# A gated mix of linear attention and a ReLU layer: the engines' programs written without a block

## The chip, the cores and the metric

The kernel runs on one core of a Trainium2 chip. Five engines work side by side, each with a program of its own: TensorE (PE) multiplies matrices, VectorE (DVE), ScalarE (ACT) and GpSimd (POOL) do the elementwise work and the reductions, and SyncE (SP) issues transfers. They meet through semaphores. ACT issues transfers too. The metric is the device time of one execution in microseconds.

## The reference

The input x has 2048 rows of 512. Two branches are computed from it and mixed with a gate for each row:

```
g = sigmoid((x * gate_w).sum(-1))
q, k, v = x @ wqkv, in 32 heads of 16
phi(t)  = concat(softmax(t @ w_phi), softmax(-(t @ w_phi)))     per head, for q and k
kv = phi(k)^T v ;  z = sum of phi(k)
a  = (phi(q) kv) / (phi(q) z + 1e-6) @ wo
b  = relu(x @ w1) @ w2                                          w1: 512 x 1376
out = g * a + (1 - g) * b
```

All inputs and the output are bf16.

## The kernel before

**Tiling.** The 2048 rows are 16 tiles of 128, in four chunks of 512. x stands transposed in SBUF (XT): the first chunk is turned by TensorE, the other three by transposing loads. The hidden layer HT is computed 512 rows at a time in 11 pieces of the hidden width (L397, L403, L409), and ACT applies the ReLU as it empties PSUM (L460). The projections of q and k are first folded with w_phi (L374) and then made two tiles at a time (L502). DVE takes maxima and minima, POOL subtracts them, ACT takes the exponential, DVE sums it, POOL normalizes. v is L482, the state kv is L563. The second half runs tile by tile: the attention's numerator and denominator (L606), a transposing transfer, eleven matmuls with w2 (L628) and four with wo (L634) into the same PSUM bank, one eviction scaled with the gate (L679), one store (L682). The last tile is cut into columns 0 to 351 and 352 to 511, with matmuls on L649 and L660: ACT evicts and stores the first part (L667, L673), DVE evicts the second part (L670) and SP stores it (L673).

**What sets the order.** Each piece of work is a task with a name, an engine and the tasks that it depends on. The order of the tasks on each engine is written out by hand in `ORDER`. `emit` walks an engine's list, puts a wait (L144) ahead of a task where a semaphore has to reach a value, writes the task's instructions and lets the last one count the engine's semaphore up. A transfer has a semaphore of its own, which reaches 16 when it has landed.

**Around the programs.** Before the kernel's function is called, the program object has already written a preamble (the profile shows it under L732): POOL writes four small constants, and all engines meet in a barrier. The function ends with five programs, one for each engine, written inside a block (`nc.Block()`). A block gives every engine a section of its own, which the engine enters with a branch and leaves with a branch to a common end. At that end each engine drains, and all engines meet in a barrier; the profile shows these records under L188, the line of the function itself. In SP's section, `emit` is followed by waits for the stores of the last tiles: stores 9 to 14 (L700) and the two stores of tile 15 (L702). Earlier stores have been waited for by the tasks that reuse their buffers.

A barrier of this kind goes so: SP, ACT, PE and DVE each drain and count one semaphore up; POOL drains, waits until that semaphore is at 4, and sets a second semaphore; the others wait for that and count it down.

Of the kernel before, what the change touches and what calls it, by code (L numbers as in the profile page):

```python
# [148 lines left out]
def bass_gated_mix__linear_kernel_hedgehog__dense_activation_relu__prompt_kernel(  # L149
# [17 lines left out]
    NT = S // P  # L167
# [13 lines left out]
    NPH, NOM, NOT, NOS = 7, 3, 4, 5  # L181
# [6 lines left out]
    with ExitStack() as es:  # L188
        E = es.enter_context
# [52 lines left out]
        g = _Graph()  # L242
# [444 lines left out]
        order = g.schedule()  # L687
        g.number(order)
        sems = {e: nc.alloc_semaphore(f"s_{e}") for e in ENGINES}
        for t in g.tasks.values():  # L690
            if t.dma:
                sems[t.sem] = nc.alloc_semaphore(f"d_{t.name}")
        block = E(nc.Block())

        @block.sync
        def _(q):
            g.emit("sp", q, order, sems)

            for m in range(NT - NOS - 2, NT - 1):
                q.wait_ge(sems[f"st{m}"], 16)  # L700
            for hf in range(2):
                q.wait_ge(sems[f"st{NT - 1}_{hf}"], 16)  # L702

        @block.gpsimd
        def _(q):
            g.emit("pool", q, order, sems)

        @block.scalar
        def _(q):
            g.emit("act", q, order, sems)  # L710

        @block.vector
        def _(q):
            g.emit("dve", q, order, sems)

        @block.tensor
        def _(q):
            g.emit("pe", q, order, sems)


# [26 lines left out]
```

## Time and profile before

| | |
|---|---|
| device time, median of 3 runs | 151.53 us (151.14, 151.53, 152.31) |
| span of the profiled execution, first to last instruction | 150.2 us |
| the profiled execution's own time | not given beside the span; the median is 1.33 us above the span |
| PE busy | 145.2 us (97%) |
| DVE, POOL, ACT busy | 113.4, 109.4, 92.2 us |
| granted clock of TensorE | 1.000 |

Busy times count work on the engine's data path. Waits on semaphores, branches, drains and the issuing of transfers are done by an engine's sequencer and are not counted as busy; views of a single source line list them with their durations and starts. A name with a q behind it (SPq, ACTq) is a sequencer.

### The profile page before, as it was taken

To read this page: it belongs to the slowest core of one execution; us is meant where nothing else is said; L and a number is where in the kernel's file an instruction comes from. 1 tells how busy PE (TensorE), PEld (TensorE's weight loads), DVE (VectorE), ACT (ScalarE), POOL (GpSimd) and SP (SyncE) were. 2 spreads that over 40 slices of the span, in tenths; PEclk is the share of its full clock that TensorE was granted. 3 is DMA by queue.
4 is the path that set the end of the run, shared out by engine and by line. 5 is a ranking of instruction groups with operands and counts; after the bars stand their busy time and mean duration, and the time that the engine had idled before them with its cause. 6 is when DMAs were issued, how large, how long until landed. Compare 5 with 4: busy or idle time off the path is not lost.

```text
span 150.2 us, 2515 instructions
## 1 busy us (share of the span) xinstructions
PE 145.2 (97%) x944; PEld 74.2 (49%) x961; DVE 113.4 (76%) x168; ACT 92.2 (61%) x127; POOL 109.4 (73%) x71
## 2 busy tenths in 40 slices
PE   7899999999999999999999999999999999999992
PEld 3664444445554465445444545445444454454461
DVE  2433666999899949979999899999999969436301
ACT  3356769799969766698983937446546551310151
POOL 3000499999999999999999999998999791330000
PEclk9999999999999999999999999999999999999999
DMA  4999995000005602300000230476698774986251
GB/s 146 280 179 233 213 203 108 0 0 0 7 1 132 218 4 66 103 0 0 4 0 0 56 86 18 92 175 140 174 110 173 179 209 105 109 212 140 64 162 53
DMA packets 46307, 15.59 MB, mean 104 GB/s; under 512 B 39796, under 2 KB 46292, under 8 KB 46296
## 3 DMA queue, kind: packets, MB, share of 16 engines
q1 hardware_dynamic: 43560, 12.99, 42.0%
q10 hardware_dynamic: 2736, 2.45, 5.1%
q8 instruction: 7, 0.11, 0.4%
q14 instruction: 4, 0.03, 0.1%
HBM read 4.42 MB, written 2.11 MB: 43 GB/s over the span
## 4 chain that ended last, share of the span: by engine, by line
PE 93%; DMA 3%; issue 1%; ACT 1%; SPq 1%; DVE 0%
PE PS L628 24%; PE PS L397 23%; PE PS L502 18%; PE PS L482 9%; PE PS L634 9%; PE PS L563 3%; PE PS L606 3%; DMA W<-in_B_w_dram 3%; PE PS L649 2%; PE PS L374 1%; ACT HT L460 1%; PE PS L403 1%; PE PS L660 1%; SPq L272 1%; PE PS L409 0%
## 5 line engine op out<-in xcount | busy, mean ns | idle before, releaser
L542 POOL TENSOR_TENSOR TS<-PB,MX 128x1024 bf16<-128x1024 bf16 (+1 forms) x18 | 30.9, 1723 | 14.9 <-DVE MX L533 14.9
L397 PE MATMUL PS<-XT,W 128*128 128x512 bf16 (+1 forms) x156 | 38.3, 379 | 0.2
L628 PE MATMUL PS<-W,HT 128*128 128x512 bf16 (+1 forms) x160 | 37.5, 379 | 0.3
L549 DVE TENSOR_REDUCE ZB<-FT 128x128 f32<-128x2048 bf16 (+1 forms) x18 | 36.6, 2031 | 1.0 <-ACT FT L547 1.0
L547 ACT ACTIVATE FT<-TS 128x2048 bf16<-128x2048 bf16 (+1 forms) x18 | 30.9, 1718 | 7.7 <-POOL TS L542 7.5
L542 POOL TENSOR_TENSOR TS<-MN,PB 128x1024 bf16<-128x1024 bf16 (+1 forms) x18 | 30.9, 1724 | 0.8 <-DVE MN L535 0.8
L502 PE MATMUL PS<-WP,XT 128*128 128x512 bf16 x124 | 30.0, 379 | 0.2
L556 POOL TENSOR_TENSOR FT<-FT,SC 128x2048 bf16<-128x2048 bf16 (+1 forms) x9 | 29.5, 3290 | 0.0
L460 ACT ACTIVATE HT<-PS 128x512 bf16<-128x512 f32 (+1 forms) x44 | 24.7, 597 | 5.8 <-PE PS L397 4.9
L628 PEld LDWEIGHTS PS<-W,HT 128*128 128x128 bf16 (+1 forms) x165 | 15.5, 98 | 17.1
L533 DVE TENSOR_REDUCE MX<-PB 128x64 bf16<-128x1024 bf16 (+1 forms) x18 | 19.5, 1085 | 5.8 <-ACT PB L529 5.7
L397 PEld LDWEIGHTS PS<-XT,W 128*128 128x128 bf16 (+1 forms) x160 | 15.6, 101 | 16.5
L679 ACT ACTIVATE OSB<-PS,OMG 128x512 bf16<-128x512 f32 x15 | 10.2, 687 | 20.3 <-PE PS L634 20.3
L535 DVE TENSOR_REDUCE MN<-PB 128x64 bf16<-128x1024 bf16 (+1 forms) x18 | 19.3, 1084 | 2.3 <-ACT PB L529 2.3
L529 ACT ACTIVATE PB<-PS 128x1024 bf16<-128x1024 f32 (+1 forms) x18 | 16.7, 927 | 6.7 <-PE PS L502 3.8
L502 PEld LDWEIGHTS PS<-WP,XT 128*128 128x128 bf16 x128 | 12.1, 98 | 13.9 <-DVE WP L344 0.4
L579 POOL TENSOR_TENSOR FT<-FT,SR 128x1024 bf16<-128x1024 bf16 (+1 forms) x9 | 15.6, 1739 | 0.7
L482 PE MATMUL PS<-WV,XT 128*128 128x512 bf16 x62 | 16.0, 379 | 0.1
L634 PE MATMUL PS<-WO,OT 128*128 128x512 bf16 x58 | 14.2, 378 | 0.1
L615 DVE SCALAR_TENSOR_TENSOR OTM<-PS,EG,RD 128x256 bf16<-128x256 f32 x32 | 13.8, 463 | 0.2
L613 DVE RECIPROCAL RD<-PS 128x16 f32<-128x16 f32 x32 | 6.5, 235 | 9.0 <-PE PS L606 8.8
L491 ACT ACTIVATE VS<-PS 128x512 bf16<-128x512 f32 x16 | 9.6, 603 | 4.8 <-PE PS L482 4.7
(50 smaller groups left out, 97.8 us busy)
## 6 DMA issues: line engine op xcount, KB each, us to landing
out_dram<-OSB ACTq DMA_DIRECT2D x15, 128.0 KB, 2.1
W<-in_B_w_dram SPq DMA_DIRECT2D x1, 1280.0 KB, 6.7
W<-in_B_w_dram SPq DMA_DIRECT2D x1, 512.0 KB, 5.6
WV<-in_A_wqkv_dram SPq DMA_DIRECT2D x1, 512.0 KB, 4.7
WO<-in_A_wo_dram SPq DMA_DIRECT2D x1, 512.0 KB, 4.7
FT<-in_A_x_dram SPq DMA_DIRECT2D x3, 128.0 KB, 4.0
W<-in_B_w_dram SPq DMA_DIRECT2D x1, 352.0 KB, 3.9
W<-in_B_w_dram ACTq DMA_DIRECT2D x2, 128.0 KB, 3.7
```

The costliest lines, as they stand in the source:

```text
L397: last = q.matmul(PS[0:m, b, :], W1[:, j, k * P:k * P + m], XT[:, j, chunk(c)], start=(j == 0), stop=(j == ND - 1))
L460: add(f"rl{a}_{k}", "act", lambda q, a=a, k=k, b=b, rows=rows: q.activation(HT[0:rows, k, chunk(a)], PS[0:rows, b, :], ACT.Relu), (prev,), ...
L482: last = q.matmul(PS[:, 2, :], XT[:, j, m * P:(m + 1) * P], WV[:, j, :], start=(j == 0), stop=(j == ND - 1))
L502: last = q.matmul(PS[:, n, :], XT[:, j, m * P:(m + 1) * P], WP[:, s, j, :], start=(j == 0), stop=(j == ND - 1))
L533: add(f"mx_{J}", "dve", lambda q, sl=sl, w=w, i=pbg: q.tensor_reduce(MX[:, sl, 0:w * H], i, AX.X, ALU.max), (f"ev_{J}", old("t1")), dur=0. ...
L535: add(f"mn_{J}", "dve", lambda q, sl=sl, w=w, i=pbg: q.tensor_reduce(MN[:, sl, 0:w * H], i, AX.X, ALU.min), (f"ev_{J}", old("t2")), dur=0. ...
L542: add(f"{tn}_{J}", "pool", lambda q, o3=o3, a3=a3, b3=b3: q.tensor_tensor(o3, a3, b3, ALU.subtract), (f"{'mx' if sg == 0 else 'mn'}_{J}", ...
L547: add(f"ex_{J}", "act", lambda q, fs=fs, ts=ts, w=w: q.activation(FT[:, fs, 0:w * F], TS[:, ts, 0:w * F], ACT.Exp), (f"t1_{J}", f"t2_{J}", ...
L549: add(f"sm_{J}", "dve", lambda q, fs=fs, sl=sl, w=w: q.tensor_reduce(ZB[:, sl, 0:2 * w * H], FT[:, fs, 0:w * F].rearrange("p (g d) -> p g ...
L556: add(f"nm_{J}", "pool", lambda q, f3=f3, sl=sl, w=w: q.tensor_tensor(f3, f3, SC[:, sl, 0:2 * w * H].unsqueeze(2).to_broadcast([P, 2 * w * ...
L628: last = q.matmul(PS[:, ab, :], HT[0:r, k, m * P:(m + 1) * P], W2[0:r, k, :], start=(k == 0), stop=False)
L634: last = q.matmul(PS[:, ab, :], OT[:, m % NOT, t, :], WO[:, t, :], start=False, stop=(t == ND - 1))
```

## The change

The block goes. The five programs are written one after the other on the engines' own handles, behind the preamble. What each engine is told to do inside its program is the same, in the same order. On each engine the branch into the section and the branch to the common end go, and with the common end its drain and its part of the closing barrier go: four instructions fewer on each of SP, ACT, PE and DVE, five fewer on POOL. SP's waits on the stores stay, at the end of SP's program; the compiler packs the eight semaphores into four wait instructions, where before they were on four wait instructions and the branch. The opening barrier of the preamble stays.

```diff
-        block = E(nc.Block())
-
-        @block.sync
-        def _(q):
-            g.emit("sp", q, order, sems)
-
-            for m in range(NT - NOS - 2, NT - 1):
-                q.wait_ge(sems[f"st{m}"], 16)
-            for hf in range(2):
-                q.wait_ge(sems[f"st{NT - 1}_{hf}"], 16)
-
-        @block.gpsimd
-        def _(q):
-            g.emit("pool", q, order, sems)
...
-        @block.tensor
-        def _(q):
-            g.emit("pe", q, order, sems)
+        for e, q in (("sp", nc.sync), ("pool", nc.gpsimd), ("act", nc.scalar), ("dve", nc.vector), ("pe", nc.tensor)):
+            g.emit(e, q, order, sems)
+
+        for m in range(NT - NOS - 2, NT - 1):
+            nc.sync.wait_ge(sems[f"st{m}"], 16)
+        for hf in range(2):
+            nc.sync.wait_ge(sems[f"st{NT - 1}_{hf}"], 16)
```

More of the change, by code (lines that the diff above doesn't have):

```diff
@@ L692, in bass_gated_mix__linear_kernel_hedgehog__dense_activation_relu__prompt_kernel @@
                 sems[t.sem] = nc.alloc_semaphore(f"d_{t.name}")
-        block = E(nc.Block())
-        @block.sync
-        def _(q):
-            g.emit("sp", q, order, sems)
-            for m in range(NT - NOS - 2, NT - 1):
-                q.wait_ge(sems[f"st{m}"], 16)
-            for hf in range(2):
-                q.wait_ge(sems[f"st{NT - 1}_{hf}"], 16)
-        @block.gpsimd
-        def _(q):
-            g.emit("pool", q, order, sems)
-        @block.scalar
-        def _(q):
[L710 to L714, printed above, removed]
-        @block.tensor
-        def _(q):
-            g.emit("pe", q, order, sems)
+        for e, q in (("sp", nc.sync), ("pool", nc.gpsimd), ("act", nc.scalar), ("dve", nc.vector), ("pe", nc.tensor)):
[4 more added lines that the diff above has]
+            nc.sync.wait_ge(sems[f"st{NT - 1}_{hf}"], 16)
 _INS = ['A_x', 'A_wqkv', 'A_w_phi', 'A_wo', 'B_x', 'B_w1', 'B_w2', 'gate_w']
```

## The prediction

> **What bounds the kernel now.** I read the page's sums first, then the chain that ended last, and then three answers on the two ends of the span, because the change touches nothing between them.
>
> ```profile
> span 150.2 us, 2515 instructions
> PE 145.2 (97%) x944; PEld 74.2 (49%) x961; DVE 113.4 (76%) x168; ACT 92.2 (61%) x127; POOL 109.4 (73%) x71
> PE 93%; DMA 3%; issue 1%; ACT 1%; SPq 1%; DVE 0%
> ```
>
> PE is busy for 97% of the span and makes up 93% of the chain. The chain in order of time shows where it is not PE:
>
> ```profile
> 0.67 0.07 issue
> 0.74 0.41 SPq L272
> 1.15 0.07 issue
> 1.21 0.41 SPq L272
> 1.62 0.05 issue
> 1.67 4.06 DMA W<-in_B_w_dram
> ...
> 5.87 0.60 PE PS L403 x4
> ...
> 146.44 0.89 PE PS L660 x8
> 147.33 0.03 issue
> 147.35 0.38 DVE OSB L670
> ```
>
> The reader is to see three stretches. Up to 0.67 us the opening barrier of the engines is under way (the preamble, which both kernels have). From there to 5.87 SP issues loads and PE waits for the third of them. From 5.87 to 147.33 PE works with hardly a gap. The chain stops at 147.35 + 0.38 = 147.73, yet the span is 150.2: some 2.5 us at the end belong to no compute engine. The busy times by stretch confirm it:
>
> ```profile
> 0.74:5.87 5.13, 4.70 (x26) 2.33 (x27) 1.72 (x4) 2.05 (x3) 1.25 (x4) 1.00 0.70 214
> 5.87:147.30 141.43, 140.53 (x918) 71.91 (x935) 111.32 (x163) 89.83 (x124) 107.99 (x63) 1.00 0.48 102
> 147.30:150.20 2.90, 0.01 (x1) 0.00 (x0) 0.38 (x1) 0.33 (x1) 0.00 (x0) 1.00 0.15 45
> ```
>
> After the length of the stretch the columns are PE, weight loads, DVE, ACT, POOL, the granted clock, the DMA share and GB/s. In the middle stretch PE is busy 140.53 of 141.43 us at a granted clock of 1.00. In the last one nothing computes but two evictions. What fills it stands in the timeline and in the issues of the last stretch:
>
> ```profile
> 147.66 0.35 ACTq L673 DMA_DIRECT2D out_dram<-OSB  x1
> 147.76 0.36 SPq L673 DMA_DIRECT2D out_dram<-OSB  x1
> ```
>
> ```profile
> q10 hardware_dynamic: 305, 0.23, 16.2%
> q1 hardware_dynamic: 144, 0.04, 4.0%
> issues: line engine op xcount, KB each, median us to landing
> out_dram<-OSB ACTq DMA_DIRECT2D x1, 88.0 KB, 1.6
> out_dram<-OSB SPq DMA_DIRECT2D x1, 40.0 KB, 1.7
> ```
>
> The last two stores land at 147.66 + 1.6 = 149.3 and 147.76 + 1.7 = 149.5 us. SP waits for them (L702), and only then comes the block's end (L188):
>
> ```profile
> L702 SPq EVENT_SEMAPHORE  x2: 28/28/28, 149.3 to 149.5; - x2
> ```
>
> ```profile
> L188 POOLq EVENT_SEMAPHORE  x2: 17/17/17, 149.7 to 149.8; - x2
> L188 POOLq DRAIN  x1: 1166/1166/1166, 131.7 to 131.7; - x1
> L188 PEldq DRAIN  x1: 1757/1757/1757, 145.6 to 145.6; - x1
> L188 DVEq DRAIN  x1: 422/422/422, 147.4 to 147.4; - x1
> L188 ACTq DRAIN  x1: 153/153/153, 148.0 to 148.0; - x1
> L188 SPq COMPARE_BRANCH  x1: 33/33/33, 149.5 to 149.5; - x1
> L188 SPq DRAIN  x1: 13/13/13, 149.7 to 149.7; - x1
> L188 ACTq EVENT_SEMAPHORE  x1: 17/17/17, 149.9 to 149.9; - x1
> L188 DVEq EVENT_SEMAPHORE  x1: 21/21/21, 149.9 to 149.9; - x1
> L188 PEldq EVENT_SEMAPHORE  x1: 51/51/51, 149.9 to 149.9; - x1
> L188 SPq EVENT_SEMAPHORE  x1: 17/17/17, 150.1 to 150.1; - x1
> ```
>
> In each row stand the shortest, median and longest duration in ns and the first and last start. SP is the last to arrive at the closing barrier, at 149.7: the other four had drained at 132.8 (131.7 + 1.166), 147.4, 147.8 and 148.2. Of these rows, then, only SP's road from 149.5 to 150.2 is on the path that sets the end.
>
> **The change part by part.**
>
> *The five opening branches.* Each engine's program ends its preamble with a jump into the block. In the trace the barrier's release on SP ends at 0.67 and the first load is issued at 0.74: a gap of 0.07 us that would hold the branch. Between the first and the second load, where no branch stands, the gap is also 0.07 (1.15 to 1.21). There is no branch record of any engine at the start either; SP's of L188 is the only one I find. So I cost the opening at nothing. Its bounds are 0 and the whole gap of 0.07 us, a gain that would pass fully to the end, since SP's issues head the chain and PE has no slack from 5.87 on (141.43 − 140.53 = 0.9 us idle in all). SP and ACT would lose the same branch, so their loads keep their order. The other side would be a load that starts earlier into transfer engines already 0.70 busy in that stretch, which can make the gain zero but hardly a loss.
>
> The Trainium skill, "Advanced Engine Details and Errata", section Control Flow Timing, gives about 51 ns for an unconditional branch. The trace disagrees for the start, where nothing is left of the 0.07 us once the ordinary gap between two issues is taken off. By the page the opening would give an estimated 0.05 us more.
>
> *The waits on the stores.* They stay, but pair differently. Before, SP has eight semaphores to wait for in five instructions, the last of them (store 9) on the branch itself; after, four instructions hold two each. A wait on two takes 28 ns in the rows of L702. The last one in the changed kernel waits for the same late landing (149.5) as L702's second one now, so it again ends at 149.5. Nothing is queued behind these waits on SP. Store 9 has landed before: tile 14's eviction waits for it too (it takes over the buffer of tile 9), ahead of ACT's last store at 147.66. Its wait costs nothing in either place. No wait is added on the other engines.
>
> *The closing branch, drain and barrier.* They go. Step by step on SP: branch and drain from 149.5 to 149.7, some 0.2 us, of which 0.033 + 0.013 are the instructions themselves; POOL's gathering of the four and its release, from 149.7 to the others' starts at 149.9, 0.2 us; SP's own release comes at 150.1, 0.2 to 0.3 us after the other engines'. To the end of the span that is 150.2 − 149.5 = 0.7 us. The view of SP's waits has the part after its drain as one number:
>
> ```profile
> SPq L188 <- SPq L188: 0.5, 1, 0.5
> ```
>
> Nothing hides these 0.7 us, as all five engines stand in them: the stores have landed and no compute is left. And nothing is late next inside the span, because the four other engines end before 148.3, over a microsecond ahead of SP. The span should thus end with SP's last wait, at 149.5.
>
> *What lies around the span.* The page gives the profiled execution's span but no time of its own; the median of 151.53 is 1.33 us above the span of 150.2, and no view shows those 1.33 us. I take them as a constant that begins when SP is done. Bounds: of the 0.7, the 0.3 by which SP is late in its release may be SP's own slowness after it wakes, and come back in the first thing it does after the span (gain 0.4); or the whole meeting of the engines is done over again outside (gain 0). On the other side the four engines could do their part of the 1.33 us early (gain 0.7 + 1.33 = 2.0). I stay at 0.7, the nearest row.
>
> The Trainium skill, "Runtime: NRT & Kernel Launch", section The launch sequence, says that after the kernel a synchronization of all engines follows that the runtime adds, some 1.5 us long, and then a reset of semaphores. No run here shows it. By that page the block's barrier is one of two in a row, and dropping it saves its own length and no more, an estimated 0.7 us, with no early reset.
>
> **Sum**: 0 (opening) + 0 (waits) − 0.7 (closing) = a span of 149.5 and, with the 1.33 us around it, 150.8 us: 0.46% less. That is below 1%, about what a measurement of this kernel tells from no change (the runs of before alone lie between 151.14 and 152.31).
>
> **The rivals.**
>
> *A: the meeting is only moved.* The engines still have to be gathered before the time is stopped, and the closing barrier's 0.5 us after SP's drain are paid after the span. For it: SP is late by 0.2 to 0.3 where nothing of the kernel holds it. Against it: nothing in these rows is work that anyone needs. It gives 151.0 to 151.5. If the compiler or the runtime put a closing of its own in place of the block's, so that the change doesn't do what it says, it is the same 151.5.
>
> *B: the four engines finish what follows under the stores.* POOL could enter it 17 us early, PE, DVE and ACT 1.3 to 2 us early (149.5 against 147.4 to 148.2). If most of the 1.33 us is each engine's own tidying, it disappears: 149.5 to 150.3 us, at the edge of it over 1% faster. Against it: SP is the last and must do its own part after 149.5.
>
> *C: slower, by loading of program code.* The page and an answer for a stretch late in the kernel show transfers of kind "instruction":
>
> ```profile
> q8 instruction: 7, 0.11, 0.4%
> q14 instruction: 4, 0.03, 0.1%
> ```
>
> ```profile
> q8 instruction: 1, 0.02, 3.4%
> ```
>
> Seven took 0.4% of 16 × 150.2 us, some 1.4 us each; the single one between 127 and 130.5 us took 3.4% of 16 × 3.5 = 1.9 us. Now SP stands 0.5 us at the barrier, and code that comes after can be fetched meanwhile. Without the barrier it runs on at once; and with two branches and the closing gone, every engine's program is shorter, so borders between loaded pieces fall elsewhere. If SP's next piece is asked for only when SP gets there, one load replaces the barrier: 1.4 to 1.9 minus 0.7 makes 152.2 to 152.7; two in a row, on two engines that hand on to each other, 154.1 at most. It decides from the point where the load takes longer than the 0.7 saved. Against it: between 146 and 150.2 us the queues in the rows above are q10 and q1 alone, so SP jumped to the block's end with no load at all, and it stands in waits from 148.2 on, long enough for a load.
>
> The same section's neighbour in that page of the Trainium skill, Instruction fetch mechanics, warns that a taken branch out of the loaded window stalls on a fetch. That would add to the gain, by an estimated load of 1.4 us. The trace speaks against it for the one branch that it shows, as no instruction queue is listed around 149.5.
>
> **How the numbers follow.** The forecast (gain 0.4 to 0.8, 150.7 to 151.1) has 0.68; A 0.12; B 0.13; C 0.07. The time is the forecast's, 150.8. The range runs from 150.0, in the middle of B, to 151.6, over all of A; it leaves out half of B, at 149.5 to 150.0, and C, with room for the scatter of before's runs. Over 1% faster is below 150.0: half of B and some scatter of the forecast, 0.13. Over 1% slower is above 153.0: two loads in a row in C, and scatter, 0.05. Within 1%: 0.82.
>
> **What would show it.** In the changed kernel's trace: no record on the function's own line for branch, drain or barrier after the last store; SP's last record a wait on two semaphores of about 28 ns near 149.5; a span of 149.4 to 149.6; the first load still 0.07 us after the opening barrier; PE's stretch from first dense matmul to last within 0.2 us of 141.4; no instruction load after 146 us. If the span falls by 0.7 and the time doesn't, A holds; if the time falls by far more than the span, B; if the span ends later with SP's wait records spread out, or an instruction packet stands there, C. I am wrong altogether if PE's stretch changes length, which nothing in the diff should do.

## The result, and the profile after

The changed kernel takes 151.25 us (median of 22 runs, 150.58 to 151.90), the kernel before 151.96 us (22 runs, 151.14 to 152.43). The ratio is 0.9957, with a 95% interval of 0.9944 to 0.9970: 0.43% less, where 0.46% was forecast. The median of before is 0.43 us higher than the one from three runs that the prediction started from, so both times stand higher by about that; the difference, 0.71 us, is the 0.7 of the prediction.

The page of the changed kernel has a shorter span and nearly the same busy times:

```profile
span 149.8 us, 2503 instructions
PE 145.8 (97%) x944; PEld 74.8 (50%) x961; DVE 113.6 (76%) x168; ACT 92.1 (62%) x127; POOL 109.4 (73%) x71
```

The two ends of its chain in order of time:

```profile
0.67 0.07 issue
0.74 2.90 DMA FT<-in_A_x_dram
3.63 0.05 issue
3.68 1.04 PE PS L350 x8
...
146.75 0.89 PE PS L660 x8
147.64 0.02 issue
147.67 0.38 DVE OSB L670
```

The opening is what it was: 0.07 us from the barrier to the first load. The end of PE's work is at 147.64, 0.31 later than before, and everything behind it is later by as much. The last stretch, by the timeline, and then SP's waits and what is left after them:

```profile
147.97 0.35 ACTq L673 DMA_DIRECT2D out_dram<-OSB  x1
148.08 0.36 SPq L673 DMA_DIRECT2D out_dram<-OSB  x1
```

```profile
L699 SPq EVENT_SEMAPHORE  x2: 28/28/28, 149.6 to 149.8; - x2
```

The reader is to see that the span now ends with SP's last wait, which starts at 149.8: behind it there is no record of any engine. From the issue of the last store to the end of the span it is 149.8 − 148.08 = 1.7 us, against 150.2 − 147.76 = 2.4 before. That is the 0.7 us.

**A second measure.** Each execution has a time and a span. Their difference, "time minus span", is what lies around the span, and it varies little: 1.50 to 1.61 us over 30 runs of the kernel before and 1.35 to 1.60 over 22 of the changed one, while the spans themselves scatter by over a microsecond (149.0 to 150.4 in the same 22 runs). So the spans' medians and the time minus span tell more than the time alone:

| | span, median | time minus span, median |
|---|---|---|
| before (30 and 31 runs beside the experiments) | 150.4 | 1.56 and 1.55 |
| after (22 runs) | 149.8 | 1.51 |

### The profile page after: what moved, and what is told of

Its sections match the earlier page's. It is cut to its first block, busy times and chain, and to the rows that moved or that the text cites. A ratio compares the mean times of both kernels' runs of the same rounds, so it can differ in the third digit from the quotient of the medians.

```text
span 149.8 us, 2503 instructions
## 1 busy us (share of the span) xinstructions
PE 145.8 (97%) x944; PEld 74.8 (50%) x961; DVE 113.6 (76%) x168; ACT 92.1 (62%) x127; POOL 109.4 (73%) x71
## 4 chain that ended last, share of the span: by engine, by line
PE 95%; DMA 2%; ACT 1%; issue 1%; DVE 0%
PE PS L628 24%; PE PS L397 23%; PE PS L502 18%; PE PS L482 9%; PE PS L634 9%; PE PS L563 3%; PE PS L606 3%; DMA FT<-in_A_x_dram 2%; PE PS L403 2%; PE PS L649 2%; PE PS L374 1%; PE PS L350 1%; ACT HT L460 1%; PE PS L660 1%; PE PS L409 1%
```

## The experiments

All of them start from the changed kernel, the last one from the kernel before; each computes the whole reference. The first four ran side by side on one chip, the last four on another; before ran beside both. Its medians there are 151.97 us both times.

### The changed kernel again

> The changed kernel once more, beside the other three, as their common measure and for a second trace. Expected: ratio to before 0.9957 within 0.0015; span near 149.8, its last record a wait of SP; time minus span again 1.5 us. If the first 3 us of loading differ from trace to trace by some 0.3 us with the same issue times, the difference of the two first traces in that stretch is scatter and no work of the change.

Measured: 151.30 us (12 runs), ratio 0.9951 (0.9929 to 0.9973), span 149.8, time minus span 1.47. Its chain begins in another way:

```profile
0.74 0.41 SPq L272
1.15 0.06 issue
1.21 0.42 SPq L272
1.63 0.05 issue
1.68 4.67 DMA W<-in_B_w_dram
6.36 0.14 issue
6.49 0.60 PE PS L403 x4
```

With the loads issued at the same times as in before (0.74, 1.21, and the third at 1.68 against 1.67), the third one lands 0.6 us later. The end of PE's work moves with such landings: 147.33, 147.64 and, in this trace, 147.9. In the three traces that is scatter of the loading. It explains why a single trace has its span 0.3 us off the forecast.

### One barrier, without a block

```diff
             nc.sync.wait_ge(sems[f"st{NT - 1}_{hf}"], 16)
+        nc.all_engine_barrier()
```

> The changed kernel with one barrier of all engines written behind SP's waits: the meeting is back, the block and its branches are not. Theory, the meeting of the engines is what was saved: ratio to before back to 1.000 within 0.0015, span 0.5 to 0.7 us longer than without it. Rival, the branches were what cost (SP's into the end of the block, and the five at the opening): the ratio stays at 0.996 to 0.997, as the barrier without branches costs 0.2 us or less.

Measured: 152.00 us (12 runs), ratio 1.0013 (0.9978 to 1.0047). The meeting takes the gain back, and no branch is needed for that. But the span's median is 150.15, shorter than before's 150.4, and time minus span is 1.83, longer than before's 1.56. SP stands in the meeting for less time than in before (0.5):

```profile
SPq L701 <- PEq L701: 0.2, 1, 0.2
```

So the time is as expected, and the way in which it divides isn't. This asked for the last experiment below.

### Five barriers

```diff
+        for _ in range(5):
+            nc.all_engine_barrier()
```

> The same with five barriers in a row, to read the price of one meeting from four more. By the closing meeting in the trace of before (0.5 us from SP's drain to its release): 4 x 0.5 = 2.0 us over one barrier, ratio to before 1.013; at 0.7 us each 2.8 us and 1.018. Rival, much of the first one's price is that SP or another engine comes out of it late, and a meeting of engines that stand there already costs 0.2 to 0.3 us: 0.8 to 1.2 us more, ratio 1.005 to 1.008.

Measured: 153.54 us (7 runs), ratio 1.0092 (1.0058 to 1.0127); span 151.5, time minus span 1.99. Four more meetings cost 1.54 us over one, 0.39 each: between what the two theories gave. SP's releases in the trace are 1.8 us apart from first to last, 0.44 each on average:

```profile
L702 SPq DRAIN  x5: 7/7/121, 149.1 to 150.7; - x5
L702 SPq EVENT_SEMAPHORE  x5: 17/17/17, 149.2 to 151.0; - x5
```

The four steps between them are not alike: by the starts in the trace file, which has nanoseconds, they are 0.76, 0.33, 0.33 and 0.36 us. In the first of them SP's drain begins only 0.47 us after its release; why, the trace does not show. A meeting of engines that stand there already thus costs about 0.33 us, near what the rival gave, and 0.4 with the slow one averaged in. The 0.7 of the block's end is more than either.

### The four other engines held, without a barrier

```diff
+        done = nc.alloc_semaphore("s_done")
+        nc.sync.sem_inc(done, 1)
+        for q in (nc.gpsimd, nc.scalar, nc.vector, nc.tensor):
+            q.wait_ge(done, 1)
```

> The changed kernel, but POOL, ACT, DVE and PE each end with a wait for a semaphore that SP counts up behind its waits on the stores: no drain, no gathering, but the four leave the program after SP, as in before. If what counts is only the span: span longer by 0.1 to 0.2 us (SP's count and the four waking), time minus span unchanged at 1.5, ratio 0.9967. Rival, engines that leave early also shorten what follows the span: time minus span rises to about 1.7, time 0.3 to 0.4 us over the changed kernel, ratio 0.998.

Measured: time minus span 1.93 (12 runs, 1.80 to 2.08), against 1.47 beside it: what follows the span takes 0.46 us longer when the four leave after SP, with no drain and no gathering. The time, 151.40 us, ratio 0.9966 (0.9943 to 0.9989), is only 0.1 above the changed kernel's, since the spans of this program happen to be shorter (149.55, with SP's additional work in them). The trace has no work that could make them shorter; its two waits of L699 stand at 149.7 and 149.9, as in the others, and its own execution was a long one (151.92). I count this as scatter from program to program, which no run here shows, and read the time minus span alone. By the time alone this run would show next to no loss.

### PE held, POOL held

The same edit for one engine, `nc.tensor` or `nc.gpsimd`.

> The changed kernel, but PE alone ends with a wait for a semaphore that SP counts up with its last wait on the stores; POOL, ACT and DVE leave early. Read by two measures: span, and time minus span (1.5 us in the changed kernel, 1.92 with all four held). Theory, what follows the span passes through the engines one after the other with PE at the beginning of the line: PE alone costs most of it, time minus span 1.75 to 1.9. Rival, it takes whichever engine is late at the same price: a quarter of the 0.42, so 1.6. Rival, another engine is the one that counts: 1.5.

> The same with POOL held instead of PE. Theory of a line that begins with PE: POOL stands further back in it, time minus span 1.6 to 1.7. Rival, POOL is the slow one by itself: 1.8 to 1.9 and PE less. Rival, equal shares: 1.6 for both.

Measured: with PE held 151.92 us (10 runs), ratio 0.9991 (0.9964 to 1.0017), time minus span 1.69; with POOL held 152.04 us (10 runs), ratio 1.0001 (0.9977 to 1.0025), time minus span 1.97 (1.89 to 2.01). POOL's whole record behind SP's last wait is this:

```profile
L703 POOLq EVENT_SEMAPHORE  x1: 17/17/17, 149.7 to 149.7; - x1
```

One wait of 17 ns on one engine, and by the time the whole gain is gone. By time minus span it costs 0.46 us; the rest lies in the spans, whose medians (150.05, and 150.3 with PE held) differ from program to program by more than the traces show work for. The prices that went with the line fail: PE costs 0.2, POOL 0.45 to 0.5, as much as all four together (1.93). POOL's rival is the one that holds: POOL is slow by itself. The line itself stands in the traces, with PE at its head (see the account). DVE and ACT were not tried alone.

### The waits on the stores at the end of PE

```diff
-            nc.sync.wait_ge(sems[f"st{m}"], 16)
+            nc.tensor.wait_ge(sems[f"st{m}"], 16)
...
-            nc.sync.wait_ge(sems[f"st{NT - 1}_{hf}"], 16)
+            nc.tensor.wait_ge(sems[f"st{NT - 1}_{hf}"], 16)
```

> The changed kernel with the waits on the stores at the end of PE's program in place of SP's; SP leaves with its last store. No count from SP to another engine is in the way here. Theory of a line that begins with PE: time minus span as with PE held, 1.75 to 1.9, and so 0.3 us slower than the changed kernel, ratio to before 0.998. Rival, the place of the waits is indifferent: time minus span 1.5, ratio 0.9955.

Measured: 151.93 us (10 runs), ratio 0.9978 (0.9950 to 1.0006), span 150.05, time minus span 1.88 (1.83 to 1.94). The place of the waits isn't indifferent: on SP they are cheaper by 0.37 us of time minus span. That the value is above the 1.69 of PE held, though PE ends last in both, I can't account for.

### The block with its branch freed of the wait

```diff
                 q.wait_ge(sems[f"st{NT - 1}_{hf}"], 16)
+            q.nop(nofuse=True)
```

In the trace the eight waits now stand in four records of 28 ns ahead of the branch, the last of them on the new line:

```profile
L703 SPq EVENT_SEMAPHORE  x1: 28/28/28, 149.8 to 149.8; - x1
```

> The kernel before, with its block, its branches and its closing barrier, but with SP's waits on the stores closed off ahead of the branch, so that four instructions hold them all and the branch to the end holds none. Theory, SP's late release in before (0.2 to 0.3 us after the other engines') comes of that one branch: without a wait on it SP is released with the others, the span is 0.3 us shorter (150.1), time minus span grows from 1.56 to 1.83 as with one barrier and no block, and the time is unchanged, ratio 0.999 to 1.001. Rival, the block's end itself makes SP late: span and time minus span as in before.

Measured: 151.96 us (10 runs), ratio 0.9995 (0.9974 to 1.0017); span 150.1, 0.3 shorter than before's; time minus span 1.82 (1.80 to 1.89), 0.27 longer. The records of the block's end:

```profile
L188 SPq DRAIN  x1: 7/7/7, 149.9 to 149.9; - x1
L188 SPq EVENT_SEMAPHORE  x1: 17/17/17, 150.1 to 150.1; - x1
L188 ACTq EVENT_SEMAPHORE  x1: 17/17/17, 150.1 to 150.1; - x1
L188 PEldq EVENT_SEMAPHORE  x1: 51/51/51, 150.1 to 150.1; - x1
```

There is no branch record on SP any more, and SP is released with the others. In before, the branch that carried a wait cost SP some 0.3 us inside the span, and the time nothing: other engines were still on the way by then, as time minus span shows and the account makes plain.

### The account

"Tail" is from the start of SP's (or PE's) second wait on the stores of tile 15 to the end of the time: what is left of the span there by the trace, and the median time minus span. The views give starts to 0.1 us; the two decimals are from the trace files.

| | span left | time minus span | tail |
|---|---|---|---|
| before | 150.17 − 149.46 = 0.71 | 1.56 | 2.27 |
| block, branch without a wait | 150.16 − 149.78 = 0.38 | 1.82 | 2.20 |
| one barrier, no block | 150.17 − 149.85 = 0.32 | 1.83 | 2.15 |
| four held | 150.05 − 149.88 = 0.17 | 1.93 | 2.10 |
| POOL held | 149.67 − 149.54 = 0.13 | 1.97 | 2.10 |
| PE held | 149.65 − 149.48 = 0.17 | 1.69 | 1.86 |
| waits on PE | 150.25 − 150.19 = 0.05 | 1.88 | 1.93 |
| after | 149.81 − 149.78 = 0.03 | 1.51 | 1.54 |

The start rows of the last wait in the experiments that the table needs:

```profile
L699 SPq EVENT_SEMAPHORE  x2: 28/28/28, 149.7 to 149.9; - x2
```

```profile
L702 SPq EVENT_SEMAPHORE  x2: 28/28/28, 149.6 to 149.8; - x2
```

The first is that of one barrier (four held has the same), the second that of the block with the plain branch. From before to after the tail loses 0.73 us, what was measured. Of the steps between, taking the block and the barrier's instructions away and still holding the engines saves only 0.17; letting the engines go, and POOL above all, saves 0.56.

**What stands behind the span.** The views end with the last instruction, but the trace files also hold the changes of the semaphores, and these go on. Semaphore 2, which does not change while the kernel works, changes nine times. Then nearly all semaphores from 7 to 255, those of the stores among them, change once more, and then semaphore 2 changes nine times again. Call the two series of nine the first and the second passing. In us from the end of the span:

| | first passing ends | second passing | time minus span of the same execution |
|---|---|---|---|
| after | 0.31 | 1.13 to 1.49 | 1.45 |
| PE held | 0.55 | 1.33 to 1.69 | 1.72 |
| waits on PE | 0.54 | 1.36 to 1.71 | 1.90 |
| four held | 0.78 | 1.56 to 1.92 | 1.87 |
| POOL held | 0.82 | 1.61 to 1.96 | 1.97 |
| one barrier, no block | 0.80 | 1.62 to 1.97 | 1.85 |
| block, branch without a wait | 0.80 | 1.62 to 1.97 | 1.84 |
| before | 0.52 | 1.34 to 1.70 | not known, the median is 1.56 |

From the end of the first passing to the end of the second it is 1.14 to 1.18 us in every row, and the time, counted from the start of the span, ends near the second's end: within 0.05 us in after and where engines are held, 0.12 to 0.18 off in the other three that have a time. So what a held engine costs is what it adds to the first passing: 0.51 us for POOL and 0.24 for PE, against 0.46 and 0.18 in the medians. That passing goes from engine to engine. In after, with SP alone late, four of its nine changes come before the span's end and the fifth 0.15 us behind it; with POOL held two come before and the third at 0.53; with PE held the first stands at 0.19. So PE is first, POOL third and SP fifth. From the end of its last record to its change POOL takes 0.53 to 0.57 us, PE 0.19 to 0.24, SP in after 0.15. Why POOL takes so long stays open. In before POOL's change stands at 0.24 and the fifth, SP's, at 0.30, both behind SP's late release, which ends the span: that is why the late release cost the time nothing.

The device times alone follow the tails less closely: four held has 151.40 us with a tail of 2.10, PE held 151.92 with 1.86. Their median spans are 149.55 and 150.3, though in both traces the wait on the last store begins 0.17 us ahead of the end; why they lie apart is not shown. Before and after do agree with their tails, and came out alike each time they were measured (151.96, 151.97 and 151.97; 151.25 and 151.30).

## Why the prediction was right, and where it wasn't

**The opening at nothing: right.** The gap of 0.07 us ahead of the first load stands in the changed kernel's chain again. The estimate of 0.05 us by the Trainium skill ("Advanced Engine Details and Errata", section Control Flow Timing) finds no row in either trace.

**The waits on the stores: right.** The last one takes 28 ns and ends with the landing of the same store, 1.7 us after its issue in both kernels.

**The closing branch, drain and barrier at 0.7: right as a term.** The spans' medians are 150.4 and 149.8, 0.6 apart; in the two traces, from the last store's issue, it is 0.7. No record on the function's own line is left, and the dense part of PE's work is what it was. The sign given for it, a stretch within 0.2 us of 141.4, failed as it was written: from 5.87 to the last matmul it is 141.77, with 140.85 us busy against 140.53:

```profile
5.87:147.64 141.77, 140.85 (x921) 72.19 (x936) 111.45 (x163) 89.79 (x124) 107.99 (x63) 1.00 0.47 100
```

The reason is the loading ahead of it. PE's first work on loaded data (L350) begins at 3.68, where it began at 3.35 in before, because its load of x landed later. L409 then begins at 7.63 against 7.30, and the last matmul ends at 147.64 against 147.33, so behind the loading PE's work has the same length. The moment 5.87 was no sharp border to begin with: the prediction's own row has PE busy for 4.70 of the 5.13 us ahead of it. And the forecast of a span of 149.4 to 149.6 was too narrow for a single trace.

**What lies around the span, "a constant that begins when SP is done": wrong, and without effect on the sum.** First in size: 1.33 was a median of three runs less the span of one execution whose own time isn't given; over 61 runs it is 1.55. Then in kind: it isn't a constant. It is 1.51 when the four engines have left early, 1.69 with PE late, 1.97 with POOL late, and it doesn't begin with SP when SP alone is late. Two errors cancelled, which was luck. The 0.3 us by which SP was late in the barrier were no gain, as the block with the plain branch shows (span −0.3, time minus span +0.27, time unchanged): that is rival A's mechanism, in part. And engines that leave early shorten what follows: rival B's mechanism, in part, some 0.3 to 0.5 us. Each was given a chance of about 0.12 as a case of its own; they came together, and the time fell where the plain sum had it. In the trace of before what follows waits for POOL until 0.24 us behind the span, not for SP.

**Rival C, loading of code: not at the end of the span.** The queues that moved anything from 146 us to the end of the changed kernel are the two of the stores:

```profile
q10 hardware_dynamic: 419, 0.34, 26.1%
q1 hardware_dynamic: 144, 0.04, 4.4%
```

Behind the span the traces of both kernels hold one more packet of kind "instruction", 8 KB on q14. It begins at 150.79 in before and at 151.06 in after, 1.33 and 1.28 us after the start of SP's last wait on tile 15, so it comes as late after the stores in both. Where the waits stand on PE no such packet is on record.

What the Trainium skill says in "Runtime: NRT & Kernel Launch", section The launch sequence, of a synchronization of all engines behind the kernel and then a reset of semaphores agrees in its order with the changes of semaphores behind the span. Its 1.5 us for the synchronization does not agree: the first passing ends 0.31 us behind the span in after and 0.82 with POOL held. "No run here shows it" held for the views, but not for the trace file of before. The gain was not the length of the doubled barrier alone, as I had taken from it.

## What to carry to other kernels

A closing barrier of all engines behind a kernel that already waits for its stores costs about 0.7 us here and buys nothing; programs written straight behind the preamble do without it. What counts is which engine leaves last: let SP hold the last waits, and let POOL and PE run out of their programs early. For an effect of half a microsecond, take the profiled span and the time minus span apart over many runs, since the loading at the start alone moved the end by up to 0.6 us between the traces.

## What the runs showed of the hardware that I had not expected

- An engine that leaves the program last costs differently by its kind: with SP last, 1.5 us pass from the span's end to the end of the time; with PE also late 1.7 (1.9 where PE itself waits for the stores), with POOL also late 2.0.
- A branch that carries a wait appears as a record of its own on SP (33 ns) and is followed by a release 0.2 to 0.3 us later than that of the other engines; the branches without a wait leave no record in any of the traces.
- A barrier of all five engines in a row with others costs 0.39 us by the time; in the trace three of four cost 0.33 to 0.36, one 0.76.
- Behind the last instruction a count passes from engine to engine, PE first, POOL third, SP fifth. POOL passes it on 0.53 to 0.57 us after its last record, PE after 0.19 to 0.24.
- SP's third load, issued at the same time to within 0.01 us, took 4.06 us in one execution and 4.67 in another, and moved the end of the kernel with it.
